# Attention and two MLPs on one core: the first weights' decoding stages are written at named steps of attention

## The chip, the cores and the metric

The kernel runs on one core of a Trainium2 chip. The metric is the device time of one execution in microseconds (us). Before the change it is 678.7 us, the median of three runs (677.99 to 679.68).

## The reference

Sliding-window attention with four sink keys (2 batches, 8 heads, 768 positions, 64 wide), then two MLPs on the 1536 tokens, each with its own nonlinearity between two matrix products. Both MLPs' weights arrive as 64-bit floats.

```python
scores = scale * np.matmul(q, k.transpose(0, 1, 3, 2))
keep = is_sink | in_window                      # 4 sinks, window of 128
scores = np.where(keep, scores, -1000000000.0)
a = np.exp(scores - np.max(scores, axis=-1, keepdims=True))
a = a / (np.sum(a, axis=-1, keepdims=True) + 1e-09)
attn = np.matmul(a, v)                          # -> x: 1536 tokens x 512
h = x @ w_in;   x = (h - np.tanh(h)) @ w_out                      # 512 -> 2048 -> 512
h = x @ w2_in;  x = (h * np.clip(h + 3.0, 0.0, 6.0) / 6.0) @ w2_out
```

## The kernel before

**Chunks.** The tokens are worked in three chunks of 512. `rest` walks a chunk's 64 MLP steps; between them it writes the attention of the next chunk. Only the first chunk's attention has no MLP beside it: `startup` writes it ahead of everything.

**Attention.** A chunk has four head pairs; (c, m) is head pair m of chunk c. For each, `score` multiplies queries and keys of four blocks for two heads on TensorE (`ps_a<-qk`); VectorE masks the scores and takes their minimum (`sc,mn`), and ScalarE takes the exponential (`sc<-sc,mn`, eight instructions per head pair). `soft` takes the reciprocal of the sums (`rs`) and scales on VectorE, the sinks (`sk`) on GpSimd. `turn_sink` and `turn_p` transpose on TensorE; ScalarE copies out (`pskT`, `p`), GpSimd makes `px` from `p`, VectorE makes the other head's `px`. `mix` multiplies by the values (`ps_a<-pskT,vsk` and `ps_a<-px,v`), and ScalarE and VectorE write the two parts `xh` and `xl` of the MLP's input. `ticks` places these pieces in 14 steps; head pair m starts at step 2m.

**Weights.** An MLP step uses one group of 128 x 512 weights; two groups are a pair, 32 pairs a chunk. In the first chunk a pair passes through stages: `w_load` (1 MB from memory into `raw`, 4 buffers), `w_scale` (ScalarE, `dec<-raw`), `w_exponent` (VectorE, a shift of `dec`), `w_sign` (ScalarE, two instructions into `r`, the first from the low words, L127, the second from the high words, L129), `w_round` (VectorE, `dec<-dec,r`), `w_keep` (0.5 MB back to memory for the later chunks) and `w_split` (GpSimd makes `wh`, VectorE makes `wl`). Four `dec`, two `r` and four `wh`/`wl` buffers limit how far a stage runs ahead.

**MLP.** A step of the first kind (`ps_h`) is 12 matmuls of 512 columns: four parts of `xh`/`xl` (one per head pair), times `wh`, `wh`, `wl`. `gate` then makes `th` (ScalarE), the difference (VectorE), `gh` (ScalarE) and `gl` (VectorE). A step of the second kind (`ps_y`) is 12 matmuls on `gh`/`gl`.

**What sets the order.** `banded` opens a block with `schedule_with_timeline_sim=True`: a scheduler reorders the written instructions on each engine by its own estimate of when operands are ready; each engine then runs its list strictly in that order. `tc.keep_in_program_order(ins)` pins an instruction behind the one written just before it on its engine. Before, the loads and `w_scale` of the first six pairs are pinned; the low words (L127) and the exponentials are not. `startup` inserts four loads and, near the end of the list of pieces, twelve half steps of `w_step`.

**SyncE.** All transfers but the first values are issued by SyncE in one order. Each issue also waits until the transfer eight issues earlier has landed, since eight completion semaphores are used in turn.

Of the kernel before, what the change touches and what calls it, by code (L numbers as in the profile page):

```python
# [12 lines left out]
U32 = mybir.dt.uint32  # L13
ACTF = mybir.ActivationFunctionType
# [30 lines left out]
class Mlp:  # L45
# [74 lines left out]
    def w_sign(self, p):  # L120


        if p >= PAIRS:
            return
        raw = self.raw.pop(p)
        r = self.rr[p] = self.r_p.tile([128, 1024], I32, tag="r", name="r")
        self.nc.scalar.activation(out=r, in_=raw[:, :, 0].bitcast(U32), func=ACTF.Copy, scale=2.0 ** -29)  # L127
        upper = r.bitcast(F16).rearrange("p (n two) -> p n two", two=2)[:, :, 1]
        self.nc.scalar.activation(out=upper, in_=raw[:, :, 1].bitcast(F32), func=ACTF.Copy, scale=2.0 ** -100)  # L129

# [264 lines left out]
class BandAttention:  # L395
# [55 lines left out]
    def score(self, it, i):  # L451
        nc = self.nc
        s = self.st[it]
        nq, off = len(s["qb"]), len(s["kb"]) - len(s["qb"])
        j = s["qb"][i][1]
        if i == 0:
            s["sc"] = self.s_p.tile([128, 2, nq, SLOT], F32, tag="sc", name="sc")
            s["mn"] = self.s_p.tile([128, 2, nq], F32, tag="mn", name="mn", bufs=3)
            s["sm"] = self.s_p.tile([128, 2, nq], F32, tag="sm", name="sm", bufs=3)
        e = off + i  # L460
        first = e if j == 0 else e - 1
        banks = []
        for a in range(2):
            qk = s["qk"][64 * a:64 * (a + 1)]
            ps = self.bank("s")
            w = SLOT * (e + 1 - first)
            nc.tensor.matmul(  # L467
                out=ps[:, 0:w], lhsT=qk[:, e, 0:128], rhs=qk[:, first:e + 1, 128:KEYS], start=True, stop=True
            )
            banks.append(ps)  # L470
        for a, ps in enumerate(banks):
            if j > 0:
                nc.vector.copy_predicated(out=ps[:, 0:128], mask=self.own_keep, data=ps[:, SLOT:SLOT + 128])
            sc, mn = s["sc"][:, a, i, :], s["mn"][:, a, i:i + 1]
            nc.vector.tensor_tensor_reduce(  # L475
                out=sc, in0=ps[:, 0:SLOT], in1=self.mask[min(j, 2)], scale=self.scale, scalar=3.0e38,
                op0=ALU.add, op1=ALU.min, accum_out=mn,
            )
            nc.scalar.activation(  # L479
                out=sc, in_=sc, func=ACTF.Exp, scale=-1.0, bias=mn, accum_out=s["sm"][:, a, i:i + 1]  # L480
            )

    def soft(self, it):
        nc = self.nc
        s = self.st[it]
        sc = s["sc"]
        rs = self.s_p.tile(list(s["sm"].shape), F32, tag="rs", name="rs")
        nc.vector.tensor_scalar(out=rs, in0=s["sm"], scalar1=1.0e-9, scalar2=None, op0=ALU.add)
        nc.vector.reciprocal(out=rs, in_=rs)
        over = lambda t, r: r.unsqueeze(len(r.shape)).to_broadcast(list(t.shape))  # L490
        sinks = sc[:, :, :, 128:SLOT]
        s["sk"] = self.s_p.tile(list(sinks.shape), F32, tag="sk", name="sk")
        nc.gpsimd.tensor_tensor(out=s["sk"], in0=sinks, in1=over(sinks, rs), op=ALU.mult)
        for a in range(2):
            p = sc[:, a, :, 0:128]
            (nc.vector if self.wide else nc.gpsimd).tensor_tensor(out=p, in0=p, in1=over(p, rs[:, a]), op=ALU.mult)
# [302 lines left out]
def banded(mlp, at):  # L799

    tc = mlp.tc
    with tc.block(schedule_with_timeline_sim=True):
        startup(mlp, at)
        at.wide = False
        rest(mlp, at)


def startup(mlp, at):
    first = [p for t in at.ticks(0) for p in t]
    for n in range(4):  # L810
        first.insert(1 if n == 0 else first.index((at.begin, (0, 3))) + n, (mlp.w_load, n))
    warm = [(p, h) for p in range(-6, 0) for h in range(2)]
    for n, p in enumerate(first):
        p[0](*p[1:])
        left = len(first) - 1 - n
        while warm and left < 0.8 * len(warm):
            mlp.w_step(*warm.pop(0))


def rest(mlp, at):  # L820
# [82 lines left out]
```

## Time and profile before

| What | Value |
|---|---|
| median of 3 runs | 678.7 us |
| the profiled execution: time, span | 677.2 us, 675.4 us |
| TensorE busy with matmuls | 637.6 us (94% of the span) |
| VectorE, ScalarE, GpSimd busy | 403.0, 362.5, 104.6 us |
| TensorE's mean granted clock | 0.99 |

TensorE is busy in nearly all of the span; what can be won is the time in which it waits, and that lies in the first 63 us, before the MLP's matmuls run without a break. Some 1.8 us lie outside the span. Busy times of TensorE count overlapping ends, so the start-to-start distance of matmuls tells more than their durations.

### The profile page before, as it was taken

The page shows a single profiled execution, that of the slowest core. Times are in us where ns is not written, and L with a number is a line of the kernel's source. Part 1 is how long each engine was busy: PE and PEld are TensorE (multiplying, and loading weights), DVE is VectorE, ACT ScalarE, POOL GpSimd, SP SyncE. Part 2 cuts the span into 40 slices and gives each one's busy share as a digit, 9 for nine tenths or more (in the row PEclk, how much of TensorE's full clock was granted, in tenths as well). Part 3 has the DMA queues.
Part 4 walks back from the last instruction along what each step waited for, and adds up shares of the span by engine and source line. Part 5 has one row for each costly group of instructions (what it writes and reads, how often), then busy time and mean ns, then how long its engine had stood idle before and what let it go on. Part 6 is the DMA issues. An engine that isn't in the chain of part 4 may idle for free.

```text
span 675.4 us, 8172 instructions
## 1 busy us (share of the span) xinstructions
PE 637.6 (94%) x2924; PEld 490.3 (73%) x2924; DVE 403.0 (60%) x721; ACT 362.5 (54%) x608; POOL 104.6 (15%) x108
## 2 busy tenths in 40 slices
PE   2488999999899999999999999999999999999995
PEld 2355777776577787887776777778788888888884
DVE  4379999878797755365555465444354444455431
ACT  1469989878878633254444454444354443454421
POOL 1025131434352421000102020201000000000000
PEclk9987999999999999999999999999999999999999
DMA  9879999768568731333312221113133323221001
GB/s 145 254 175 304 385 364 357 282 233 284 205 220 294 231 113 32 111 129 117 110 63 80 72 99 63 62 63 126 63 125 124 102 87 112 76 69 56 0 1 67
DMA packets 38897, 98.87 MB, mean 146 GB/s; under 512 B 17856, under 2 KB 25024, under 8 KB 30656
## 3 DMA queue, kind: packets, MB, share of 16 engines
q1 hardware_dynamic: 34624, 97.22, 43.4%
q10 hardware_dynamic: 4224, 1.05, 1.1%
q8 instruction: 25, 0.41, 0.3%
q14 instruction: 24, 0.20, 0.1%
HBM read 78.33 MB, written 19.92 MB: 145 GB/s over the span
## 4 chain that ended last, share of the span: by engine, by line
PE 74%; DVE 10%; DMA 5%; ACT 5%; issue 2%; SPq 0%; POOL 0%; ACTq 0%; DVEq 0%
PE ps_y L175 11%; PE ps_h L175 11%; PE ps_h L176 11%; PE ps_h L177 11%; PE ps_y L176 11%; PE ps_y L177 11%; DMA raw<-in_w_dram 4%; PE ps_a L554 3%; DVE dec L135 3%; PE ps_a L467 3%; DVE dec L118 2%; DMA keep<-dec 2%; DVE wl L152 2%; ACT r L127 2%; ACT dec L107 1%
## 5 line engine op out<-in xcount | busy, mean ns | idle before, releaser
L176 PE MATMUL ps_y<-gl,wh 128*128 128x512 f32 x384 | 151.2, 394 | 0.0
L177 PE MATMUL ps_y<-gh,wl 128*128 128x512 f32 x384 | 149.9, 391 | 0.0
L175 PE MATMUL ps_y<-gh,wh 128*128 128x512 f32 x384 | 144.3, 400 | 0.0
L152 DVE TENSOR_TENSOR wl<-raw,wh 128x1024 fp32r<-128x1024 f32 x64 | 79.3, 1239 | 58.5 <-ACT wh L151 57.7
L151 ACT CAST wh<-raw 128x1024 fp32r<-128x1024 f32 x64 | 67.2, 1050 | 48.9 <-PE ps_y L176 41.2
L175 PEld LDWEIGHTS ps_y<-gh,wh 128*128 128x128 f32 x384 | 71.8, 188 | 21.6 <-issue 5.7
L176 PEld LDWEIGHTS ps_y<-gl,wh 128*128 128x128 f32 x384 | 72.1, 188 | 17.3 <-issue 2.6
L177 PEld LDWEIGHTS ps_y<-gh,wl 128*128 128x128 f32 x384 | 72.1, 188 | 15.7 <-issue 0.3
L175 PE MATMUL ps_h<-yh,wh 128*128 128x512 f32 x192 | 76.6, 403 | 2.4 <-ACT yh L243 1.2
L175 PE MATMUL ps_h<-xh,wh 128*128 128x512 f32 x192 | 77.4, 405 | 0.1
L177 PE MATMUL ps_h<-xh,wl 128*128 128x512 f32 x192 | 76.1, 397 | 0.4 <-DVE wl L152 0.3
L176 PE MATMUL ps_h<-yl,wh 128*128 128x512 f32 x192 | 76.3, 398 | 0.1
L176 PE MATMUL ps_h<-xl,wh 128*128 128x512 f32 x192 | 76.4, 398 | 0.0
L177 PE MATMUL ps_h<-yh,wl 128*128 128x512 f32 x192 | 75.9, 396 | 0.0
L233 ACT ACTIVATE th<-ps_h,three 128x512 f32<-128x512 f32 x48 | 32.8, 685 | 70.1 <-PE ps_h L177 69.9
L235 DVE SCALAR_TENSOR_TENSOR th<-th,ps_h 128x512 f32<-128x512 f32 x48 | 32.8, 684 | 53.2 <-ACT th L233 53.1
L479 ACT ACTIVATE sc<-sc,mn 128x132 f32<-128x132 f32 x96 | 38.1, 398 | 38.9 <-DVE mn L475 28.8
L149 POOL CAST wh<-dec 128x1024 fp32r<-128x1024 f32 x32 | 44.5, 1393 | 92.7 <-PE ps_y L176 60.2
L467 PE MATMUL ps_a<-qk 64*128 64x264 f32 (+1 forms) x192 | 44.6, 453 | 13.5 <-DVE delta L739 9.4
L227 ACT ACTIVATE th<-ps_h 128x512 f32<-128x512 f32 x48 | 28.5, 593 | 45.4 <-PE ps_h L177 38.9
L229 DVE TENSOR_TENSOR th<-ps_h,th 128x512 f32<-128x512 f32 x48 | 33.0, 687 | 31.7 <-ACT th L227 31.6
L127 ACT ACTIVATE r<-raw 128x1024 int32<-128x1024 uint32 x32 | 36.8, 1151 | 24.7 <-DVE dec L135 15.2
(77 smaller groups left out, 879.7 us busy)
## 6 DMA issues: line engine op xcount, KB each, us to landing
raw<-in_w_dram SPq DMA_DIRECT2D x32, 1024.0 KB
raw<-keep SPq DMA_DIRECT2D x32, 1024.0 KB
keep<-dec SPq DMA_DIRECT2D x32, 512.0 KB
out_dram<-ob SPq DMA_DIRECT2D x12, 256.0 KB
qk<-in_qkv_dram SPq DMA_DIRECT2D x8, 325.0 KB
qk<-in_qkv_dram SPq DMA_DIRECT2D x8, 260.0 KB
qk<-in_qkv_dram SPq DMA_DIRECT2D x8, 195.0 KB
v<-in_qkv_dram SPq DMA_DIRECT2D x8, 160.0 KB
```

The lines of the kernel that those rows point to most:

```text
L127: self.nc.scalar.activation(out=r, in_=raw[:, :, 0].bitcast(U32), func=ACTF.Copy, scale=2.0 ** -29)
L149: nc.gpsimd.tensor_copy(out=wh, in_=src)
L151: nc.scalar.copy(out=wh, in_=src)
L152: nc.vector.tensor_sub(out=wl, in0=src, in1=wh.bitcast(F32))
L175: mm(out=ps, lhsT=wh, rhs=ah, start=first, stop=False)
L176: mm(out=ps, lhsT=wh, rhs=al, start=False, stop=False)
L177: mm(out=ps, lhsT=wl, rhs=ah, start=False, stop=last)
L229: nc.vector.tensor_sub(out=u, in0=ps, in1=th)
L233: nc.scalar.activation(out=th, in_=ps, func=ACTF.Relu, bias=self.three)
L235: nc.vector.scalar_tensor_tensor(out=u, in0=th, scalar=6.0, in1=ps, op0=ALU.min, op1=ALU.mult)
L467: nc.tensor.matmul(out=ps[:, 0:w], lhsT=qk[:, e, 0:128], rhs=qk[:, first:e + 1, 128:KEYS], start=True, stop=True)
L479: nc.scalar.activation(out=sc, in_=sc, func=ACTF.Exp, scale=-1.0, bias=mn, accum_out=s["sm"][:, a, i:i + 1])
```

## The change

`startup` no longer packs the first weights' stages into half steps near the end of attention's list: a table, `WARM`, names for each stage the step of attention's pipeline behind which it is written (the first entries: pair 0's load behind step 0, its `scale` behind step 5, its `sign` behind step 6). In `w_sign` the low words of the first four pairs are pinned, and in `score` the exponentials of head pair (1, 0), the first of the second chunk.

```diff
-        self.nc.scalar.activation(out=r, in_=raw[:, :, 0].bitcast(U32), func=ACTF.Copy, scale=2.0 ** -29)
+        ins = self.nc.scalar.activation(out=r, in_=raw[:, :, 0].bitcast(U32), func=ACTF.Copy, scale=2.0 ** -29)
+        if p < 4:
+            self.tc.keep_in_program_order(ins)
...
-            nc.scalar.activation(
+            ins = nc.scalar.activation(
                 out=sc, in_=sc, func=ACTF.Exp, scale=-1.0, bias=mn, accum_out=s["sm"][:, a, i:i + 1]
             )
+            if it == (1, 0):
+                self.tc.keep_in_program_order(ins)
...
+WARM = (
+    (0, "load", 0), (3, "load", 1), (4, "load", 2), (4, "load", 3),
+    (5, "scale", 0), (5, "exponent", 0), (6, "sign", 0), (7, "round", 0),
...
 def startup(mlp, at):
-    first = [p for t in at.ticks(0) for p in t]
-    for n in range(4):
-        first.insert(1 if n == 0 else first.index((at.begin, (0, 3))) + n, (mlp.w_load, n))
-    warm = [(p, h) for p in range(-6, 0) for h in range(2)]
-    for n, p in enumerate(first):
-        p[0](*p[1:])
-        left = len(first) - 1 - n
-        while warm and left < 0.8 * len(warm):
-            mlp.w_step(*warm.pop(0))
+    warm = list(WARM)
+    for n, t in enumerate(at.ticks(0)):
+        for p in t:
+            p[0](*p[1:])
+        while warm and warm[0][0] <= n:
+            _, stage, pair = warm.pop(0)
+            getattr(mlp, f"w_{stage}")(pair)
```

The scheduler's lists change with it. The first place is ScalarE's start, here in the list before: sc_200 and sc_248 are the scores of head pairs (0, 0) and (0, 1), raw64_190 and raw64_271 the weights of pairs 0 and 1.

```order
L479 ACTIVATE sc_200,sm_202<-sc_200,mn_201 128x132 x4
L127 ACTIVATE r_521<-raw64_190 128x1024
L479 ACTIVATE sc_200,sm_202<-sc_200,mn_201 128x132
L129 ACTIVATE r_521<-raw64_190 128x1024
L479 ACTIVATE sc_200,sm_202<-sc_200,mn_201 128x132 x3
L479 ACTIVATE sc_248,sm_250<-sc_248,mn_249 128x132 x5
L506 COPY pskT_279<-ps_a_277 32x128
L127 ACTIVATE r_541<-raw64_271 128x1024
L479 ACTIVATE sc_248,sm_250<-sc_248,mn_249 128x132
L526 COPY p_287<-ps_a_281 128x512
L129 ACTIVATE r_541<-raw64_271 128x1024
```

The same place in the list after (sc_250 is now head pair (0, 1), sc_329 head pair (0, 2); lines 479, 506, 526 and 129 have become 481, 510, 530 and 131):

```order
L481 ACTIVATE sc_200,sm_202<-sc_200,mn_201 128x132 x8
L481 ACTIVATE sc_250,sm_252<-sc_250,mn_251 128x132 x5
L510 COPY pskT_279<-ps_a_277 32x128
L481 ACTIVATE sc_250,sm_252<-sc_250,mn_251 128x132
L530 COPY p_287<-ps_a_281 128x512
L481 ACTIVATE sc_250,sm_252<-sc_250,mn_251 128x132 x2
L107 ACTIVATE dec_311<-raw64_190 128x1024
L481 ACTIVATE sc_329,sm_331<-sc_329,mn_330 128x132 x3
L562 CAST xh_173<-ps_a_353 128x512
L481 ACTIVATE sc_329,sm_331<-sc_329,mn_330 128x132
L127 ACTIVATE r_350<-raw64_190 128x1024
```

Both low-word instructions have left the exponentials of (0, 0) and (0, 1); the first weights' instruction is now the `scale` of pair 0, behind all 16 of them.

The second place is ScalarE's list between the last head pair's copy of `p` and the first `gh` of the MLP. Before, in full from `xh` of head pair (0, 3) on (raw64_554, 583 and 643 are pairs 5, 6 and 7):

```order
L558 CAST xh_173<-ps_a_562 128x512
L129 ACTIVATE r_722<-raw64_554 128x1024
L107 ACTIVATE dec_621<-raw64_554 128x1024
L127 ACTIVATE r_776<-raw64_583 128x1024
L129 ACTIVATE r_776<-raw64_583 128x1024
L227 ACTIVATE th_604<-ps_h_591 128x512
L127 ACTIVATE r_822<-raw64_643 128x1024
```

After, from that copy of `p` on (raw64_273, 275 and 514 are pairs 2, 3 and 4):

```order
L530 COPY p_542<-ps_a_536 128x512
L107 ACTIVATE dec_547<-raw64_273 128x1024
L562 CAST xh_173<-ps_a_558 128x512
L127 ACTIVATE r_573<-raw64_273 128x1024
L131 ACTIVATE r_573<-raw64_273 128x1024
L107 ACTIVATE dec_578<-raw64_275 128x1024
L107 ACTIVATE dec_581<-raw64_514 128x1024
L229 ACTIVATE th_604<-ps_h_591 128x512
L127 ACTIVATE r_618<-raw64_275 128x1024
L229 ACTIVATE th_638<-ps_h_623 128x512
L127 ACTIVATE r_672<-raw64_514 128x1024
L232 CAST gh_605<-th_604 128x512
```

At `xh` of (0, 3) the list before is at pair 5, the list after at pair 2; eight instructions stand between that `xh` and the first `gh`.

The third place is SyncE's list ahead of pair 6's load. Before (v_68 and v_69 are the values of the second chunk's head pairs 2 and 3, vsk its sinks, dec_481 and dec_499 pairs 0 and 1, raw64_583 pair 6):

```order
L288 DMA v_68<-in_qkv_dram 128x3x64 x2
L91 DMA raw64_526<-in_w64_dram 128x2048
L288 DMA v_68<-in_qkv_dram 128x2x64 x2
L139 DMA keep_179<-dec_481 128x1024
L91 DMA raw64_554<-in_w64_dram 128x2048
L447 DMA vsk_61<-in_vs_dram 4x4x64 x2
L139 DMA keep_179<-dec_499 128x1024
L447 DMA vsk_61<-in_vs_dram 4x4x64 x2
L91 DMA raw64_583<-in_w64_dram 128x2048
```

After (dec_439 is pair 1, raw64_576 pair 5, raw64_583 again pair 6):

```order
L141 DMA keep_179<-dec_439 128x1024
L91 DMA raw64_576<-in_w64_dram 128x2048
L290 DMA v_68<-in_qkv_dram 128x3x64 x2
L290 DMA v_68<-in_qkv_dram 128x2x64 x2
L449 DMA vsk_61<-in_vs_dram 4x4x64 x8
L290 DMA v_69<-in_qkv_dram 128x3x64 x2
L290 DMA v_69<-in_qkv_dram 128x2x64 x2
L91 DMA raw64_583<-in_w64_dram 128x2048
```

Pair 6's load now stands behind all eight sink transfers and the values of the last head pair; pair 1's load has gone ahead of the keys of (0, 3) (not shown).

## Rows read from the trace of the kernel before

**Rows 1.** Timeline of ScalarE: start, duration, instruction, idle before it and its releaser.

```profile
22.57 1.12 ACT L127 ACTIVATE r<-raw 128x1024 int32<-128x1024 uint32 x1 [7.98 <-DMA raw<-in_w_dram]
...
31.80 1.13 ACT L127 ACTIVATE r<-raw 128x1024 int32<-128x1024 uint32 x1 [1.51 <-DMA raw<-in_w_dram]
...
33.69 1.35 ACT L129 ACTIVATE r<-raw 128x1024 f16<-128x1024 f32 x1
...
47.77 0.56 ACT L526 COPY p<-ps_a 128x512 f32<-128x512 f32 x1
...
50.99 4.25 ACT L107 ACTIVATE dec<-raw 128x1024 f32<-128x1024 f32 x4
...
66.34 0.59 ACT L558 CAST xh<-ps_a 128x512 fp32r<-128x512 f32 x1
...
75.61 0.63 ACT L230 CAST gh<-th 128x512 fp32r<-128x512 f32 x1
```

**Rows 2.** Timeline of TensorE, the same columns.

```profile
27.73 0.40 PE L504 MATMUL ps_a<-ident,sk 128*32 128x128 f32 x1 [8.17 <-POOL sk L493]
...
35.13 3.04 PE L554 MATMUL ps_a<-px,v 128*64 128x256 f32 x14 [2.75 <-POOL px L532]
...
49.81 1.74 PE L554 MATMUL ps_a<-px,v 128*64 128x256 f32 x16
...
55.91 2.07 PE L554 MATMUL ps_a<-pskT,vsk 32*128 32x128 f32 x8 [2.24 <-ACT pskT L506]
...
59.91 3.00 PE L554 MATMUL ps_a<-px,v 128*64 128x256 f32 x16
...
63.31 0.40 PE L175 MATMUL ps_h<-xh,wh 128*128 128x512 f32 x1
...
77.26 1.07 PE L175 MATMUL ps_y<-gh,wh 128*128 128x512 f32 x4
```

**Rows 3.** Timeline of VectorE, the same columns.

```profile
17.84 0.29 DVE L475 CUSTOM_DVE_ANT_0 sc<-ps_a,keep 128x132 f32<-128x132 f32 x1 [1.38 <-PE ps_a L467]
...
26.45 0.17 DVE L488 TENSOR_SCALAR rs<-sm 128x8 f32<-128x8 f32 x1 [8.31 <-ACT sc L479]
...
36.19 0.17 DVE L488 TENSOR_SCALAR rs<-sm 128x8 f32<-128x8 f32 x1 [3.60 <-ACT sc L479]
...
51.12 0.17 DVE L488 TENSOR_SCALAR rs<-sm 128x8 f32<-128x8 f32 x1 [0.56 <-ACT sc L479]
...
54.03 1.21 DVE L135 CUSTOM_DVE_ANT_0 dec<-dec,r 128x2048 uint16<-128x2048 uint16 x1
55.16 0.68 DVE L118 TENSOR_SCALAR dec<-dec 128x1024 int32<-128x1024 int32 x1
...
61.71 1.21 DVE L152 TENSOR_TENSOR wl<-dec,wh 128x1024 fp32r<-128x1024 f32 x1
```

**Rows 4.** Timeline of GpSimd (POOL), the same columns.

```profile
33.86 0.63 POOL L528 TENSOR_SCALAR_AFFINE_SELECT px<-p 128x512 f32<-128x512 f32 x1 [6.18 <-ACT p L526]
...
56.70 1.62 POOL L528 TENSOR_SCALAR_AFFINE_SELECT px<-p 128x512 f32<-128x512 f32 x1
```

**Rows 5.** Busy time, granted clock, DMA share of one stretch; PE is TensorE.

```profile
core 0: us, PE busy (x) PEld busy (x) DVE busy (x) ACT busy (x) POOL busy (x), PEclk, DMA share, GB/s
...
35.00:36.00 1.00, 0.87 (x4) 0.53 (x6) 0.00 (x0) 1.00 (x7) 0.08 (x1) 0.50 1.09 232
```

**Rows 6.** Waits, 56 to 120 us: engine, line, releaser: us in total, times, longest.

```profile
POOL wh L149 <- PE ps_y L176: 22.6, 6, 5.9
...
PE ps_h L177 <- DVE wl L152: 0.3, 1, 0.3
```

**Rows 7.** Timeline of SyncE's queue, the same columns.

```profile
24.28 1.54 SPq L91 DMA_DIRECT2D raw<-in_w_dram  x3
...
59.00 0.58 SPq L91 DMA_DIRECT2D raw<-in_w_dram  x1
```

**Rows 8.** Chain of waits, 10 to 80 us: start, length, what.

```profile
73.79 7.58 DMA raw<-in_w_dram
```

More of the change, by code (lines that the diff above doesn't have):

```diff
@@ L805, in banded @@
         rest(mlp, at)
-def startup(mlp, at):
-    first = [p for t in at.ticks(0) for p in t]
-    for n in range(4):
-        first.insert(1 if n == 0 else first.index((at.begin, (0, 3))) + n, (mlp.w_load, n))
-    warm = [(p, h) for p in range(-6, 0) for h in range(2)]
-    for n, p in enumerate(first):
-        p[0](*p[1:])
-        left = len(first) - 1 - n
-        while warm and left < 0.8 * len(warm):
-            mlp.w_step(*warm.pop(0))
+WARM = (
+    (0, "load", 0), (3, "load", 1), (4, "load", 2), (4, "load", 3),
+    (5, "scale", 0), (5, "exponent", 0), (6, "sign", 0), (7, "round", 0),
+    (8, "scale", 1), (8, "exponent", 1), (8, "keep", 0), (8, "split", 0), (9, "sign", 1),
+    (10, "load", 4), (10, "round", 1), (11, "keep", 1), (11, "scale", 2), (12, "exponent", 2),
+    (13, "sign", 2), (13, "load", 5), (13, "scale", 3), (13, "exponent", 3), (13, "scale", 4),
+)
+def startup(mlp, at):
+    warm = list(WARM)
[5 more added lines that the diff above has]
+            getattr(mlp, f"w_{stage}")(pair)
 def rest(mlp, at):
```

## The prediction

> **What bounds the kernel now.** I read the busy shares first: TensorE carries 94% of the span, so time can only be won where TensorE waits. The waits of TensorE over the span show where: nearly all lie before 63 us, in the first chunk's attention, which has no MLP beside it; from there its matmuls follow each other at a steady pitch. Then I read the four engines' timelines of that stretch side by side. TensorE waits 8.17 us for GpSimd's `sk` and gets it at 27.73 [rows 2]; `sk` waits for VectorE's `rs`, which itself sat 8.31 us [rows 3], and that for ScalarE, which sat 7.98 us at the low words of pair 0 until their load had landed at 22.57 [rows 1]. The exponentials that `rs` wants stand behind them in ScalarE's list. The reader is to see one wait passed on through four engines. It comes a second time, smaller: at 31.80 ScalarE reaches the low words of pair 1 after 1.51 us idle [rows 1], the copy `p` stands behind them, GpSimd's `px` waits for `p` [rows 4], and TensorE waits 2.75 us for `px` [rows 2].
>
> **The change, part by part.** All times are those of the profiled execution, 677.2 us; it is 1.5 under the median of 678.7, and I add that back at the end. I follow the head pairs' milestones and ask how much earlier each comes.
>
> *The removed waits.* In the new list all exponentials of (0, 0) stand ahead of any weights. VectorE has its next score at 17.84 + 0.29 = 18.1 [rows 3] and then `rs`; TensorE came 1.28 us after `rs` started (26.45 to 27.73), which gives 19.4, and TensorE itself was free at 27.73 - 8.17 = 19.56 [rows 2, 3]. So the first transposes start near 19.6: 8.2 us earlier. The second wait goes too: `px` of (0, 0) starts at 35.13 - 8.2 - 2.6, say 24.5. Behind `p` the high words of pair 1 (1.35 us [rows 1]) leave as well, so `rs` of (0, 1) comes at 24.4 instead of 36.19 [rows 3]: 11.8 us earlier.
>
> *What is put in their place.* Two whole pairs are now decoded inside attention. One pair costs ScalarE 4.25 / 4 + 1.13 + 1.35 = 3.5 us [rows 1], VectorE 0.68 + 1.21 + 1.21 = 3.1 us [rows 3], and a copy on GpSimd. Most of it fills time in which these engines sat, but every stage delays what stands behind it. Pair 0's `sign` (2.5 us) stands ahead of the copy `p` of (0, 1), and pair 1's load now goes ahead of the keys of (0, 3); before, both together had landed by 31.80 [rows 1, 7], so I let these keys arrive at 31.5, and TensorE's next mix waits for both: the lead falls to 9 us. Pair 0's `wl` (1.2) and pair 1's `exponent` (0.7) on VectorE and its `scale` (1.1) on ScalarE take nearly 3 more: `rs` of (0, 3) at 44.8 instead of 51.12 [rows 3], lead 6.3. Then a run of stages stands ahead of the last mix: `sign` of pair 1 2.4, `round` 1.2, GpSimd's copy (no row alone; between the 0.63 and 1.62 of another GpSimd operation [rows 4], I take 1.2), `wl` 1.2, `xl` and the two `px` 0.6 each on VectorE (by the nearest row, 0.68 with its overlap). 44.8 + 7.8 = 52.6; the mix takes 1.74 at full clock [rows 2] and `xh` 0.6 more, less 0.4 in which the first products overlap the last `px`: `xh` of (0, 3) ends near 54.5. Before, it ended at 66.34 + 0.59 = 66.9 [rows 1], behind four `scale` of 4.25 us and a slow mix: the lead is 12.4 again.
>
> *What is late next.* The list gives part of it back. Between this `xh` and the first `gh` stand eight instructions: `sign` of pair 2 (1.13 + 1.35), two `scale` (2.1), two `th` (0.6 each, by the nearest row, `gh`), two low words (2.3). That is 8.1 us with `gh` itself in the overlaps, so `gh` comes at 62.6 [rows 1]. TensorE reaches the first `ps_y`, which wants it, after only 38 matmuls of the first MLP; before, 60 had run when it started at 77.26 [rows 2]. From 63.31 to 77.26 there are 55 of them, 0.254 us each with their small waits, so the 22 missing ones are worth 5.6 us. The gain at this point, past which both orders do the same work, is 77.26 - 62.6 - 5.6 = 9.1 us. Of the 8.1 us TensorE can fill 2.6 with eleven matmuls; it waits some 5.5.
>
> *The clock.* After its wait of 2.75 us TensorE was granted 0.50 from 35 to 36 [rows 5], 1.2 of 2.4 GHz, and the mix then took 3.04 us, and again 3.00 at 59.91 behind the wait of 2.24, against 1.74 at full clock [rows 2]: 1.3 us lost each time. A wait of 5.5 us ahead of the first `ps_y` should cost as much or a little more; I take 1.5, between 0 and 2.6 (twice that row). The page "TensorE: Matmul & The Clock Gate" of the Trainium skill (section "HAM oscillation — how this bites in real kernels") says that waits between bursts of matmuls send the engine back to half its clock, and that each burst pays again. It speaks against the change here: by it the sum is the one given; did the clock stay full, 1.5 us more would be won.
>
> *Supply of weights.* Pair 6's load was issued at 59.00 [rows 7], before the last mix was through; now it stands behind eight sink transfers and four of values, which wait for that mix and for each other's landing. By my walk it is issued near 60 and wanted at 66.7. The row of such a load in the chain is 7.58 us [rows 8], which gives 67.6; I take 0.6 us lost, between 0 and 6. Before, too, `wl` was ready just in time (one wait of 0.3), and between 56 and 120 us GpSimd's copies waited 22.6 us in six waits for TensorE to free their buffers [rows 6]: the decoding catches up, and what is lost is lost once.
>
> *GpSimd beside VectorE.* `px` on GpSimd took 0.63 alone and 1.62 beside a `round` on VectorE [rows 4]. The page "GPSIMD Engine Reference" of the Trainium skill (section "1. Specifications") says that GpSimd shares its memory interfaces with VectorE and contends with instructions that have two inputs there, as `round` and `wl` have. By it the last mix, whose `px` now lies beside pair 1's `wl`, comes up to 2 us later, and the sum would be 5.0; the trace agrees where the two overlapped, but the list now puts GpSimd's copy and VectorE's `wl` one after the other, so I leave the sum as it is.
>
> *At nothing.* The pinned exponentials of (1, 0) lie beside the MLP, where TensorE has matmuls queued; without that cover a ScalarE wait there costs what the waits at 31.80 did, 1.5 us. The rest of the program has the same instructions; small shifts in it I bound by 2 us either way.
>
> Sum: 9.1 - 1.5 - 0.6 = 7.0 us. 677.2 - 7.0 = 670.2 for the profiled execution, 671.7 as a median.
>
> **The rivals.**
> *More is won.* If `gh` is not what TensorE waits for (its mix ends sooner, or ScalarE runs these eight earlier), TensorE is unbroken from `xh` at 54.5, with 27 matmuls done. Before, 27 were done 22 x 0.254 after 63.31, at 68.9: 14.4 us earlier, less 1 for the clock; 665.3. For it: TensorE has 27 matmuls to fill attention's gaps with. Against: the list is strict.
> *The weights are late.* If pair 6 lands 4 us after it is wanted, or two pairs 2 us each, TensorE waits that long with nothing else: gain 3, 675.7. For it: one completion slot in eight, and loads of 7.58 us. Against: four buffers, and the slack seen later.
> *Slower.* The same place, but as a chain: SyncE's issue of a sink waits for the landing of pair 5, the values' issue for the sinks, pair 6's for the values. If each of the three takes a load's 7.58 us, pair 6 is issued at 49 + 22.7 = 71.7 and lands at 79.3, 12.6 later than wanted: 671.7 + 12.6 = 684.3. It decides from a landing at 73.7 on (66.7 + 7.0).
> *It doesn't do what it says.* The exponentials leave the low words, but the keys of (0, 3) or the last sinks, loaded beside pair 1, become the wait of the same length: 678.7 within 1.
>
> **How the numbers follow.** The forecast (gain 4 to 10) 0.55, with a range of its own from 668.5 to 674.5; more 0.18; late weights 0.14; slower 0.07; not as it says 0.06. Eight in ten lie from 665.5 to 676.5: most of "more" and half of "late" are in, slower and no change out. Below 676.7 (faster by over 0.3%, about what a measurement of this kernel can tell from no change) lie the forecast, more, and most of late weights: 0.86. Within 0.3%: 0.07. Slower: 0.07.
>
> **What would show it.** After: no wait for a load on ScalarE before 22 us; first transposes near 19.6; `rs` of the four head pairs near 18, 24, 35 and 45; `xh` of the last near 54; TensorE waiting 4 to 6 us for `gh` near 60, with a clock of 0.50 behind it; then an unbroken pitch, and the second MLP, the later chunks and the end as before, only earlier. I am wrong if the first transposes start after 24, if TensorE waits for `wl` by more than 2 us in all after 63 us, or if the lead at 100 us differs from that at the end by more than 2 us.

## The result and the profile after

The changed kernel takes 672.12 us in the median of four runs (671.35 to 672.98), the kernel before 678.47 (677.99 to 679.68): 0.9904 of it, with a 95% interval from 0.988 to 0.9928. That is 6.35 us faster, at the predicted 671.7 and inside the range. A second series gave 0.991 (0.9882 to 0.9939). The profiled execution took 672.98 us, its span 671.3 against 675.4 before, so that the two traces lie only 4.1 us apart and hold 4 of the 6.35.

The timeline of ScalarE in the changed kernel answers [rows 1]; the columns are the same. L127 and L131 are the low and high words of a pair, L107 its scale, L530 the copy `p`, L562 `xh`, L229 `th`, L232 `gh`.

```profile
29.27 1.13 ACT L127 ACTIVATE r<-raw 128x1024 int32<-128x1024 uint32 x1
...
30.44 1.35 ACT L131 ACTIVATE r<-raw 128x1024 f16<-128x1024 f32 x1
...
32.04 0.56 ACT L530 COPY p<-ps_a 128x512 f32<-128x512 f32 x1
...
57.77 0.59 ACT L562 CAST xh<-ps_a 128x512 fp32r<-128x512 f32 x1 [7.12 <-PE ps_a L558]
58.25 1.13 ACT L127 ACTIVATE r<-raw 128x1024 int32<-128x1024 uint32 x1
59.42 1.37 ACT L131 ACTIVATE r<-raw 128x1024 f16<-128x1024 f32 x1
60.65 2.14 ACT L107 ACTIVATE dec<-raw 128x1024 f32<-128x1024 f32 x2
62.69 0.59 ACT L229 ACTIVATE th<-ps_h 128x512 f32<-128x512 f32 x1
...
65.72 0.61 ACT L232 CAST gh<-th 128x512 fp32r<-128x512 f32 x1
```

The two waits for a load, 7.98 and 1.51 us, are gone; the first low words come at 29.27 and wait for nothing. At the end stands a new one: 7.12 us for the last mix, and behind its `xh` the queue of eight instructions to `gh` that the prediction counted (two low words and the second `th` are left out above).

TensorE, the answer to [rows 2]:

```profile
19.58 0.39 PE L508 MATMUL ps_a<-ident,sk 128*32 128x128 f32 x1
...
24.58 1.51 PE L558 MATMUL ps_a<-px,v 128*64 128x256 f32 x10
...
34.18 1.84 PE L558 MATMUL ps_a<-px,v 128*64 128x256 f32 x14 [0.36 <-POOL px L536]
...
50.98 0.50 PE L177 MATMUL ps_h<-xh,wh 128*128 128x512 f32 x1 [1.59 <-POOL wh L151]
...
53.20 0.50 PE L179 MATMUL ps_h<-xh,wl 128*128 128x512 f32 x1
...
55.63 0.40 PE L179 MATMUL ps_h<-xh,wl 128*128 128x512 f32 x1
55.96 1.74 PE L558 MATMUL ps_a<-px,v 128*64 128x256 f32 x16
...
63.59 0.50 PE L177 MATMUL ps_h<-xh,wh 128*128 128x512 f32 x1 [2.81 <-POOL wh L151]
...
66.38 2.07 PE L177 MATMUL ps_y<-gh,wh 128*128 128x512 f32 x4 [1.96 <-ACT gh L232]
```

The first transposes start 8.15 us earlier, without a wait. At 50.98 TensorE has waited 1.59 us for the copy of pair 1. Eleven matmuls of the MLP (53.20 to 55.63) stand ahead of the last mix; then come the waits of 2.81 us for the copy of pair 2 and 1.96 us for `gh`.

VectorE, the answer to [rows 3], and under it GpSimd, to [rows 4]:

```profile
24.69 0.17 DVE L492 TENSOR_SCALAR rs<-sm 128x8 f32<-128x8 f32 x1
...
36.41 0.17 DVE L492 TENSOR_SCALAR rs<-sm 128x8 f32<-128x8 f32 x1 [0.91 <-ACT sc L481]
...
46.12 0.17 DVE L492 TENSOR_SCALAR rs<-sm 128x8 f32<-128x8 f32 x1 [0.56 <-ACT sc L481]
...
50.96 1.63 DVE L154 TENSOR_TENSOR wl<-dec,wh 128x1024 fp32r<-128x1024 f32 x1 [1.13 <-POOL wh L151]
...
53.72 0.67 DVE L525 TENSOR_TENSOR px<-ps_a,past 128x512 f32<-128x512 f32 x1
```

```profile
51.47 1.62 POOL L536 TENSOR_SCALAR_AFFINE_SELECT px<-p 128x512 f32<-128x512 f32 x1
```

Pair 1's `wl` ran beside GpSimd's `px`; the one took 1.63 us against 1.21 before, the other 1.62 against 0.63. The last `px` of (0, 3) is VectorE's, and it ends at 54.39.

A window of the changed kernel, the answer to [rows 5] (columns: stretch, its length, busy time of each engine, granted clock, DMA share, GB/s), then TensorE's waits from 60 to 180 us as in [rows 6], and SyncE's row for pair 6 as in [rows 7]:

```profile
64.00:71.00 7.00, 5.04 (x13) 3.66 (x12) 6.48 (x9) 6.39 (x8) 1.44 (x1) 0.51 0.91 250
```

```profile
PE ps_h L177 <- POOL wh L151: 2.8, 1, 2.8
PE ps_y L177 <- ACT gh L232: 2.5, 2, 2.0
PE ps_h L177 <- ACT yh L245: 1.8, 1, 1.8
PE ps_a L469 <- DVE th L231: 0.9, 1, 0.9
```

```profile
65.05 0.42 SPq L91 DMA_DIRECT2D raw<-in_w_dram  x1
```

From 64 us, behind the first of the two waits, the clock is 0.51 for 7 us. No wait for `wl` is in the list, although pair 6 was issued 6 us later than before. The last mix of the second chunk ends 4.8 us earlier than before (`xh` at 263.2 against 268.0), and so does the last cast of the output on ScalarE (662.9 against 667.6): in between nothing more is won. Behind that cast 0.6 us is lost again (8.4 us to the end of the span against 7.8).

A second trace of the changed kernel, of the second series, has the same waits for pair 2 and `gh` (2.8 and 2.0 us), but more stretches at half clock and its milestones 2.7 us later (last `xh` at 60.46, first `ps_y` at 69.08), and yet a span of 671.2 us. The times of single milestones below are thus good to some 3 us, not to 0.1.

Four executions of the last three experiments were disturbed (684.1 and 1061.4 us in the eighth, 680.0 in the ninth, 1260.5 in the tenth); they are left out of the times given here, and no times are read from the traces of the eighth and the tenth, which show such executions.

### The profile page after: what moved, and what is told of

The parts are those of the page before. It is cut to its first block, busy times and chain, and to the rows that moved or that the text cites. A ratio compares the mean times of both kernels' runs of the same rounds, so it can differ in the third digit from the quotient of the medians.

```text
span 671.3 us, 8169 instructions
## 1 busy us (share of the span) xinstructions
PE 637.5 (95%) x2924; PEld 489.9 (73%) x2924; DVE 399.8 (60%) x721; ACT 361.2 (54%) x608; POOL 102.4 (15%) x108
## 4 chain that ended last, share of the span: by engine, by line
PE 77%; DVE 8%; ACT 7%; issue 2%; DMA 1%; SPq 0%; POOL 0%; DVEq 0%; ACTq 0%
PE ps_h L177 12%; PE ps_y L177 12%; PE ps_h L178 12%; PE ps_h L179 12%; PE ps_y L178 11%; PE ps_y L179 11%; PE ps_a L558 4%; PE ps_a L469 3%; DVE dec L137 2%; ACT r L127 2%; DVE dec L118 2%; ACT r L131 2%; ACT dec L107 1%; PE ps_a L519 1%; DVE wl L154 1%
## 5 line engine op out<-in xcount | busy, mean ns | idle before, releaser
L229 ACT ACTIVATE th<-ps_h 128x512 f32<-128x512 f32 x48 | 28.6, 596 | 47.1 <-PE ps_h L179 37.5
L177 PEld LDWEIGHTS ps_h<-xh,wh 128*128 128x128 f32 x192 | 36.3, 190 | 18.3 <-POOL wh L151 5.3
```

Source lines behind the costliest of these rows:

```text
L177: mm(out=ps, lhsT=wh, rhs=ah, start=first, stop=False)
L229: nc.scalar.activation(out=th, in_=ps, func=ACTF.Tanh)
```

## The experiments

Each kernel was timed in five rounds beside the kernel before. My theory was that the exponentials freed from the weights are the gain and that the named steps put the decoding into idle time; the main rival, that one of the two parts does it all.

**1. The pin alone.** The kernel before with

```
-        self.nc.scalar.activation(out=r, in_=raw[:, :, 0]...
+        ins = self.nc.scalar.activation(out=r, in_=raw[:, :, 0]...
+        if p < 4:
+            self.tc.keep_in_program_order(ins)
```

> The kernel before with only the low words of the first four pairs kept behind what is written ahead of them; the stages are spread as before. Theory (the freed exponentials carry the gain, the named steps put the decoding into the time that this frees): first transposes near 19.6 and the xh of (0, 3) some 8 to 10 us earlier than 66.9, but no pair is decoded by then, so TensorE waits for weights behind it; 3 to 5 us faster than before, near 674.5. Rival (the named steps are the gain, the pin only carries attention forward into a wait for weights): within 1 us of before. Rival (the pin is all, the steps add nothing): as the changed kernel, 672.

Measured: 669.73 us, 0.9862 of before (0.9836 to 0.9888), and a second time

> The pin on the low words alone, once more, beside the two that follow. Theory (the stages that the table puts inside attention cost more than they give: TensorE's waits and its time at 0.50 of the clock from 17 to 180 us make 21 us in the changed kernel and 16 with the pin alone): 0.986 of before, 2 to 3 us ahead of the changed kernel. Rival (no difference between the two): 0.9905, as the changed kernel in both of its runs.

669.42 us, 0.9889 (0.9858 to 0.992). The rival "the pin is all" is borne out, and more: the two pairs of series put the pin alone at 0.9862 and 0.9889, the whole change at 0.9904 and 0.991. By their means that is some 2 us in favour of the pin alone. Each was timed beside the kernel before, but not beside the other, and the intervals overlap, so the sign is likely and the size not sure. ScalarE and then TensorE of the pin alone:

```profile
44.52 1.16 ACT L127 ACTIVATE r<-raw 128x1024 int32<-128x1024 uint32 x1
45.59 0.56 ACT L528 COPY p<-ps_a 128x512 f32<-128x512 f32 x1
46.05 1.13 ACT L127 ACTIVATE r<-raw 128x1024 int32<-128x1024 uint32 x1
...
51.54 0.56 ACT L560 CAST xh<-ps_a 128x512 fp32r<-128x512 f32 x1
...
60.75 1.12 ACT L107 ACTIVATE dec<-raw 128x1024 f32<-128x1024 f32 x1 [6.21 <-DMA keep<-dec]
```

```profile
47.49 3.26 PE L556 MATMUL ps_a<-px,v 128*64 128x256 f32 x16 [1.36 <-POOL px L534]
51.22 0.80 PE L177 MATMUL ps_h<-xh,wh 128*128 128x512 f32 x1 [0.48 <-POOL wh L151]
...
54.88 0.50 PE L179 MATMUL ps_h<-xh,wl 128*128 128x512 f32 x1 [2.03 <-DVE wl L154]
...
63.78 0.50 PE L179 MATMUL ps_h<-xh,wl 128*128 128x512 f32 x1 [1.96 <-DVE wl L154]
```

The last `xh` comes at 51.54, 6.2 us before that of the changed kernel. TensorE then waits for weights, but behind 64 us no more, and for `gh` not at all.

By the first `ps_y`, though, most of that lead is gone: with the same 38 matmuls done it starts at 66.69, against 66.38 in the changed kernel (67.58 against 69.08 in the second traces of both). Some of what separates them comes later, where the first MLP hands over to the second. There the kernel before waits twice, the changed kernel once, and the pin alone not at all; first the kernel before, then the changed one:

```profile
170.66 0.50 PE L175 MATMUL ps_h<-yh,wh 128*128 128x512 f32 x1 [1.19 <-ACT yh L243]
172.77 0.49 PE L175 MATMUL ps_h<-yh,wh 128*128 128x512 f32 x1 [1.18 <-DVE xl L559]
```

```profile
168.12 0.50 PE L177 MATMUL ps_h<-yh,wh 128*128 128x512 f32 x1 [1.75 <-ACT yh L245]
```

The second traces agree on this wait (1.2 us in the changed kernel, none with the pin alone). So the pin alone wins part of its time there and not in the first attention; what in its list removes that wait was not tested.

**2. The steps alone.** The changed kernel without the pin that run 1 adds.

> The changed kernel without the pin on the low words: its named steps stand, but the order now puts the low words of pairs 0 and 1 among the exponentials of (0, 0). Theory: ScalarE waits there for the first load until 22.6 as before and then for the second until about 31, so the first transposes come near 33 instead of 27.73; the decoding is done in attention all the same, which gives some of it back at the end of attention: 1 to 5 us slower than before, near 681. Rival (the named steps are the gain): at least 3 us faster than before.

Measured: 684.47 us, 1.0073 (1.0044 to 1.0101): slower than before. The direction is the theory's, the mechanism not quite: the second load had landed by 28.1, so ScalarE waited 1.17 us for it and not until 31.

```profile
22.34 1.12 ACT L127 ACTIVATE r<-raw 128x1024 int32<-128x1024 uint32 x1 [7.82 <-DMA raw<-in_w_dram]
...
28.13 1.15 ACT L127 ACTIVATE r<-raw 128x1024 int32<-128x1024 uint32 x1 [1.17 <-DMA raw<-in_w_dram]
```

The first transposes start at 27.50, as before, and the last `xh` at 69.4 against 66.3: with the waits still there, the steps lengthen attention by 3 us. That the steps are the gain is refuted.

**3. The pin on the second chunk's exponentials.** Its two lines left out.

> The changed kernel without the pin on the first exponentials of the second chunk. Theory (they lie beside the MLP, where TensorE has matmuls queued): within 1 us of the changed kernel. Rival (the pinned exponentials wait for VectorE there and hold the gh behind them, which is why the changed kernel is behind the pin on the low words alone): 2 us faster than the changed kernel.

Measured: 671.44 us, 0.9906 (0.9876 to 0.9935). The theory holds; this part of the change can't be told from nothing.

**4. The last stages ahead of the last `xh`.**

```
-    (13, "sign", 2), (13, "load", 5), (13, "scale", 3), (13, "exponent", 3), (13, "scale", 4),
+    (12, "sign", 2), (12, "load", 5), (12, "scale", 3), (12, "exponent", 3), (12, "scale", 4),
```

> The changed kernel with the stages of the thirteenth step (sign of pair 2, scale of pairs 3 and 4) written one step earlier, ahead of the last mix. They fill the 7.1 us in which ScalarE sat for that mix. Theory (the 2.8 us wait for pair 2's copy and the 2.0 us wait for gh behind attention are what is left of the loss there, because four stages stand between the last xh and gh): both waits go or shrink to under 1 us together, gh comes 3 to 4 us earlier, the half clock behind it is shorter; 3 to 4 us faster than the changed kernel, near 668.5. Rival (TensorE's weights come no faster, the wait moves to the next pair): within 1 us of 672.

Measured: 673.36 us, 0.9914 (0.9887 to 0.9942): nothing won, the rival is right. ScalarE, then TensorE:

```profile
61.16 0.58 ACT L562 CAST xh<-ps_a 128x512 fp32r<-128x512 f32 x1 [1.43 <-PE ps_a L558]
63.30 0.60 ACT L229 ACTIVATE th<-ps_h 128x512 f32<-128x512 f32 x1 [1.55 <-PE ps_h L179]
63.80 2.14 ACT L127 ACTIVATE r<-raw 128x1024 int32<-128x1024 uint32 x2
...
66.32 1.35 ACT L131 ACTIVATE r<-raw 128x1024 f16<-128x1024 f32 x1
67.53 1.11 ACT L107 ACTIVATE dec<-raw 128x1024 f32<-128x1024 f32 x1
68.53 0.61 ACT L232 CAST gh<-th 128x512 fp32r<-128x512 f32 x1
```

```profile
69.20 2.02 PE L177 MATMUL ps_y<-gh,wh 128*128 128x512 f32 x4 [2.20 <-ACT gh L232]
```

The wait for pair 2's copy is gone, but the order fills the place of the four stages with the next pairs', and `gh` comes 7.4 us behind the last `xh`, against 8.0 in the changed kernel, almost as if nothing had been moved; TensorE waits 2.2 us for it.

**5. The last mix freed.** Beside that, the first matmul of the MLP's third step is pinned.

> As the run before it, and the first matmul of the third step of the MLP is kept behind what is written ahead of it, so that eight and not seventeen MLP matmuls stand between the third and the last mix, and none of them wants pair 1. Theory: the last mix starts when its px is ready, about 54.4 instead of 55.96, and xh ends 1.5 us earlier; 1 to 1.5 us faster than that run, near 667.3, since the matmuls held back fill the wait for gh. Rival (the held matmuls are lost as cover in attention): 0 to 1 us slower than that run.

Measured: 668.9 us, 0.9861 (0.9824 to 0.9897). By the means that is 3.6 us faster than run 4, where 1 to 1.5 were expected, but the two intervals overlap, and this one reaches from 2.6 us ahead of the pin alone's first mean almost to the changed kernel's. Its trace is of an execution of 674.4 us, when four of the six took 667.9 to 669.2; there `xh` of (0, 3) came at 58.6 and not near 56. Inconclusive.

**6. One step moved.** `(6, "sign", 0), (7, "round", 0)` become `(7, "sign", 0), (8, "round", 0)`.

> The changed kernel with two steps moved: the sign of pair 0 stands behind the copy p of (0, 1) instead of ahead of it, and its round one step later. Theory (what the named steps cost is attention's own time: the xh of (0, 1) comes at 40.4 in the changed kernel and at 36.8 with the pin alone, since 2.5 us of sign and 1.2 us of round stand ahead of p and px): the xh of (0, 1) near 37, the last xh 2 to 3 us earlier than 57.8, and 1 to 2.5 us faster than the changed kernel. Rival (the delay only moves on to the next head pair, or the wait for pair 2's weights takes it back): within 1 us.

Measured: 671.8 us, 0.99 (0.9875 to 0.9926). From the first `xh` to the second it now takes 10.0 us (30.0 to 40.0) against 12.0 in the changed kernel (28.4 to 40.4) and 8.6 with the pin alone (28.1 to 36.8); the last `xh` comes at 54.9. So the price of that step in attention is real, 2 us of it; but TensorE waits 1.99 us for pair 2's copy and 2.07 for `gh` behind it, and the time is the changed kernel's within its uncertainty. The rival named this.

**7. All steps later.** Signs of pairs 0, 1 and 2 at steps 8, 11 and 12, their other stages behind.

> All stages of the first weights placed two or three steps later, where ScalarE and VectorE sit: the sign of pair 0 behind the last exponentials of (0, 2), that of pair 1 behind the p of (0, 3), and the sign of pair 2 and the scales of pairs 3 and 4 ahead of the last xh, where ScalarE waited 7.1 us. Theory (pins and steps add up once the steps fill idle time only): the xh of (0, 3) near 52, TensorE waits for weights or gh under 2 us together after it, 4 to 6 us faster than the changed kernel and 2 to 3 faster than the pin alone: 0.983 of before. Rival (the supply of weights by the loads sets the pace from 60 us on, whatever the order): as the pin alone, 0.986.

Measured: 674.38 us, 0.9937 (0.9914 to 0.9959), the highest mean of the tables with a pin, though its interval overlaps the changed kernel's. The last `xh` came at 58.85, not near 52. VectorE and TensorE show one place where the theory fails:

```profile
43.08 1.22 DVE L137 CUSTOM_DVE_ANT_0 dec<-dec,r 128x2048 uint16<-128x2048 uint16 x1 [1.52 <-ACT r L131]
44.23 0.68 DVE L525 TENSOR_TENSOR px<-ps_a,delta 128x512 f32<-128x512 f32 x1
```

```profile
45.56 3.13 PE L558 MATMUL ps_a<-px,v 128*64 128x256 f32 x14 [1.71 <-DVE px L525]
```

The round of pair 0 waits 1.52 us for its low and high words, and `px` of (0, 2) stands behind it. I had read the pauses of ScalarE and VectorE as free time; here the pause belonged to attention's own chain, and the stage that filled it pushed the chain on. Its last `xh` lies between those of the two traces of the changed kernel (57.77 and 60.46), so this explains the miss and not a loss against the changed kernel.

**8. Matmuls that nobody reads.** On the pin alone:

```
+            spare = self.mlp.ps_h.tile([128, 512], F32, tag="h", name="ps_h")
+            for n in range(FILL):
+                nc.tensor.matmul(out=spare[:, 0:128], lhsT=mms[n % 4][1], rhs=mms[n % 4][2], start=True, stop=True)
...
```

`FILL` is 8; the loop stands once behind the mix of (0, 2) and once ahead of that of (0, 3). The six repeats of the first MLP matmul are not shown.

> The pin alone, with matmuls added that nobody reads: eight small ones behind the mix of (0, 2), eight ahead of that of (0, 3), and six repeats of the first MLP matmul, all where TensorE waited between 42 and 55 us. Theory (TensorE's clock falls to 0.50 behind those waits, and 10 us at that clock cost 5.1 of the 16 us still lost there): the clock stays at 1.00 from 42 to 60, and 2 to 5 us are won against the pin alone. Rival (the clock falls all the same, or the added matmuls stand in the way of the awaited ones): within 1 us of it, or up to 2 us slower.

Measured: 673.7 us, 0.9936 (0.9912 to 0.996), by the means some 3 us slower than the pin alone in the same series (0.9889; the intervals just overlap). The theory of a gain is refuted; the rival has the direction, and the loss is larger than its 2 us. The clock did stay higher: its mean over the span was 0.989 to 0.994 in the six executions, against 0.980 to 0.991 in those of the pin alone beside it. So less was lost to the clock, and more to something else; what, isn't shown, without a trace that can be read.

**9. The weights' loads first.** On the pin alone, the second chunk's loads of keys, values and sinks are each pinned behind what is written ahead of them (`if c == 1: self.tc.keep_in_program_order(ins)`).

> The pin alone, with the second chunk's keys, values and sinks kept behind the weights' loads on SyncE, where the order had put 22 of them ahead of pair 4's load. Theory (with the pin alone that load was issued at 53.32 although its buffer came free at 48.3; ScalarE's scale waited 6.2 us for it, VectorE's exponent stood behind that and the wl of pair 1 behind the exponent, so TensorE waited 2.0 us): issued near 49, no such wait, 1.5 to 2.5 us faster than the pin alone. Rival (the second chunk's keys now come late, or ScalarE's order ahead of gh becomes the wait): within 1 us, or slower.

Measured: 669.3 us, 0.9868 (0.9845 to 0.989): the same as the pin alone. SyncE and ScalarE:

```profile
50.02 0.33 SPq L91 DMA_DIRECT2D raw<-in_w_dram  x1
51.28 0.33 SPq L141 DMA_DIRECT2D keep<-dec  x1
```

```profile
57.24 1.15 ACT L107 ACTIVATE dec<-raw 128x1024 f32<-128x1024 f32 x1 [1.11 <-DMA keep<-dec]
```

The load of pair 4 is issued at 50.02 instead of 53.32, and pair 0's decoded words go out to `keep` at 51.28 instead of 54.48. ScalarE waits 1.11 us instead of 6.21; TensorE's wait near 64 is gone from its list. The profile names the `keep` transfer as what ScalarE waited for, whose landing frees one of four decoded buffers, and not the load that I had named; both were moved by 3.3 us, so the run doesn't tell them apart. Nor is the vanished wait near 64 surely this edit's doing: the second trace of the pin alone lacks it too, at half clock, and no time was won there either. The saving can't be told from nothing here.

**10. Named steps behind attention's last copy.** On run 9, with the high words pinned too:

```
...
+    (10, "scale", 0), (10, "scale", 1), (11, "exponent", 0), (11, "exponent", 1), (11, "sign", 0), (11, "load", 4),
+    (12, "round", 0), (12, "keep", 0), (12, "split", 0), (12, "sign", 1), (12, "load", 5), (12, "scale", 2), (12, "exponent", 2),
+    (12, "round", 1), (12, "keep", 1), (12, "scale", 3), (13, "sign", 2), (13, "exponent", 3), (13, "scale", 4),
```

> The run before with the second chunk's loads behind the weights' (0.987 of before), and now a table of named steps again, but with every sign behind attention's last copy p: scales of pairs 0 and 1 ahead of the third xh, sign of pairs 0 and 1 behind the p of (0, 3), high words pinned behind low words. Theory (a stage costs nothing only where no copy, exponential or px of attention stands behind it; with the pin alone the low words of pair 0 stood ahead of that p and those of pair 1 ahead of pair 0's high words, 1.1 us each): the last xh 1 us earlier, wh and wl of pair 0 1 to 2 us earlier, no wait for them over 1 us, 1 to 2 us faster than that run: 0.985 of before, about 668. Rival (TensorE's time there is set by px and its half clock): the same as that run, within 1 us.

Measured: 665.4 us in the median of five executions, 0.9805 of before (0.978 to 0.983). This beats both kernels: its interval lies under that of the changed kernel (0.988 to 0.9928) and under run 9's. It is about 4 us ahead of run 9 where 1 to 2 were expected. Its order has `p` of (0, 3) ahead of every low word. The table and the pin on the high words came in together and were not tried apart, and without a trace that can be read it stays open where the 4 us come from.

## Why the prediction was right, and where it was not

*The removed waits*: right. First transposes near 19.6, measured 19.58; the mix on `px` of (0, 0) 24.5, measured 24.58; `rs` of (0, 1) 24.4, measured 24.69.

*What is put in their place*: half right. `rs` of (0, 3) was put at 44.8 and came at 46.12, and the last `xh` was to end at 54.5 and ended at 58.36. Of these 3.9 us, 1.3 were there at `rs` and 0.5 came with the stages behind it. The largest part, 1.6 us, is that I let the mix start when its `px` was ready, at 54.39; it started at 55.96, because the list puts eleven MLP matmuls ahead of it, and these began only at 53.20, behind TensorE's wait of 1.59 us for pair 1's copy. I had counted these matmuls only as cover for the wait for `gh`. The last 0.5 us is mostly the overlap of mix and `px` that I took off.

The contention of GpSimd and VectorE that the Trainium skill names ("GPSIMD Engine Reference", section "1. Specifications"), and that I left out of the sum, is in the trace at this very place (1.62 and 1.63 us). But it did not delay the mix: GpSimd's `px` ended at 53.09, VectorE's last, which the longer `wl` put off by 0.4 us, at 54.39, and both were ready well before the eleven matmuls were through. So the smaller sum, 5.0, that went with it lies nearer to the 4.1 between the two profiled spans than my 7.0 by luck.

*What is late next*: the right instruction, the wrong size. `gh` was to come at 62.6, ended at 66.33, and the first `ps_y` started at 66.38. From the last `xh` to `gh` it took 8.0 us where I had 8.1, so the queue was right and the late `xh` is the whole miss. The gain at that point, worked out as before, is 77.26 - 66.38 - 5.6 = 5.3 us and not 9.1: this is the term that was mis-sized, for the reason above. The wait of 5.5 us is there as 2.81 + 1.96 = 4.8, more than half of it for pair 2's copy, which I had not named.

*The clock*: mis-sized. In 7 us at 0.51 with 5.04 us of matmuls it cost 5.04 x 0.49 = 2.5 us, not 1.5, just under the upper end that I gave it. By starts it is a little less: eleven large matmuls came 0.428 us apart instead of 0.232, which is 2.2 us.

*Supply*: the load of pair 6 was issued at 65.05 and not near 60; ScalarE's scale of that pair then waited 1.91 us, by the profile for a `keep` transfer, and TensorE for no `wl` at all. 0, not 0.6.

*The rest*: 5.3 - 2.5 = 2.8 us, but the lead at the end is 4.8. Part of the 2 us between is my sizing. Both traces hold all 2924 matmuls, so 22 is exact, but without small waits large matmuls start 0.232 us apart, which makes 5.1 and not 5.6; with 2.2 for the clock the lead is 10.9 - 5.1 - 2.2 = 3.6 us. The remaining 1.2 us arise in the second chunk's attention and at its end. Counted in matmuls done (my estimate, each weighed with its usual distance), the lead is 3 to 4 us from 80 to 95 us, 2.5 to 3 at 100, near 1 at 130, and some 5 from 180 on. So it is not true that both orders do the same work past the first `ps_y`: the scheduler has placed the second chunk's attention otherwise. The lead at 100 us differs from that at the end by some 2 us, which is the edge of what I had named as a sign of being wrong; the other two signs did not come.

So the profiled executions differ by 4.1 and not 7.0, and the medians, which were predicted from them, by 6.35: the profiled execution of the changed kernel was the slowest of its four (672.98), and that of the kernel before (677.2) took less than any of its series. That the forecast of 671.7 is so close is luck; the removed waits and the place of the next one were not.

*The rivals*: "more" failed, since TensorE did wait for `gh`; "late weights" and "slower" by SyncE's chain did not happen; "not as it says" is refuted by 19.58. A rival that I did not have is the strongest finding: half of the change, the named steps, wins nothing that the pin alone does not win. With them the last `xh` comes over 6 us later, and the first `ps_y` about when it does without them.

## What to carry to other kernels

Where an engine waits in the middle of a chain of short steps, first move the long wait out of its list, and try that alone before anything is put into the room it leaves. Do not take idle time between a chain's steps for room: here stages that were put there delayed the chain (runs 6 and 7), and the fastest table had its signs behind the chain's last copy (run 10). A stage moved out of the way of a late instruction was replaced by the next stage in the order (run 4), so say what fills its place.

## What was not expected of the hardware

The same program takes different clocks. Two profiled executions of the pin alone, from 18 to 28 us (columns: stretch, length, TensorE's busy time, granted clock, DMA share, GB/s), the first and then the second:

```profile
18.00:28.00 10.00, 9.51 (x53) 1.00 0.72 205
```

```profile
18.00:28.00 10.00, 9.55 (x39) 0.51 0.73 206
```

The program is the same, and the wait ahead of the stretch 1.52 us in the one and 1.82 in the other. Over 17 to 180 us the granted clock cost 5.1 us in the first and 11.9 in the second (what it lacks of 1.00, summed over windows of 1 us), yet the spans are 667.8 and 668.4. In the second the last `xh` came 2.2 us later (53.79 against 51.54), but the first `gh` at the same time (64.35 and 64.36). TensorE's waits fell from 9.1 to 7.2 us: the wait near 64 us is gone, since slower matmuls filled it while `wl` came as before (62.48 and 62.51). In these two executions a fall of the clock in attention cost less than its rows suggest.
